# Two neighbouring positions per partition, attention in 64x64 array tiles, state product on the diagonal

## The chip, the cores and the metric

The kernel runs on one core of one Trainium2 chip. Its time is device microseconds, the median over runs. The core has five engines with queues of their own, each executed in order: PE (matrix products, with weight loads that the profile lists as PEld), DVE and ACT (elementwise work; both read PSUM), POOL (elementwise work in SBUF, and DMA issue), SP (DMA issue). They wait for one another through semaphores.

## The reference

Inputs are q, k, v of shape (4 batches, 8 heads, 768 positions, 64), one decay `lam` per head, and the weights of a two-layer network. Attention is linear with decay, and is written in blocks of 64 positions:

```python
Dmask = np.where(rel >= 0, lam[:, None, None] ** rel[None, :, :], 0.0)
...
intra = np.einsum('bhic,bhjc->bhij', qb, kb) * Dmask[None]
intra = np.einsum('bhij,bhjd->bhid', intra, vb)
inter = np.einsum('bhid,bhde->bhie', qb * lam_pow[None], kv_state)
out[:, :, sl] = intra + inter
...
kv_state = lam_block[None, :, None, None] * kv_state + np.einsum('bhsd,bhse->bhde', kb_dec, vb)
```

The result is laid out as 3072 tokens of 512 values, x, and goes through

```python
h = x @ w_in                                            # 512 -> 2048
g = np.maximum(h, 0.0) + alpha * np.minimum(h, 0.0)
return (g @ w_out).astype(np.float32)                   # 2048 -> 512
```

The block size doesn't change the result, so a kernel may take 128 positions at a time.

## The kernel before, in words

A chunk is 128 positions of all four batches, 512 tokens; there are six chunks (`sb` or `c`), and 24 units of one chunk and one batch. Heads go in pairs: two heads of 64 values fill 128 partitions, `hp` counts pairs and `hl` the head in the pair.

For each unit, `load` (L63) brings q, k and v with one position per partition, so that each partition takes eight pieces of 256 bytes, one per head. `casts` (L185) makes fp16 copies on the engines that a three-letter word names for q, k, v (A for ACT, V for DVE, G for POOL) and lets POOL make `kdec`, the decayed k. `transposes` (L204) turns k and q by eight PE transposes into one PSUM tile, copies it to `qkT`, and POOL makes the decayed queries `qdT`. `scores` (L219) is eight products of k and q into two PSUM tiles; DVE multiplies them by the decay mask into `sm` (L235). `outputs` (L238) is eight inter products of the state `R` with `qdT` (L245) and eight intra products of v with `sm` (L255) into one PSUM tile, which ACT copies to `xT`. `states` (L267) is eight products of `kdec` and v (L283); POOL scales the old state into `rd` (L273) and DVE adds (L294).

`up` (L300) makes one block of 128 of the 2048 hidden values for 512 tokens, or for half of them: four matmuls into `h_ps`, of which there are three buffers, then ACT's `m` (L314) and DVE's `g` (L317). `down` (L326) adds four of sixteen matmuls for 128 tokens into `o_ps`; after the last, ACT copies and issues the store (L343).

Nothing is reordered: the queue of each engine is the order of the calls from L399 on. That order is written by hand for chunk 0, up(0), chunk 1's attention and up(1); then `weave` (L386) mixes chunk 2's attention with down(0), and from there attention of chunk c+1 with up(c) and down(c-1). The weights `w_in` and `w_out` come in four pieces each, issued on POOL's queue and cast to fp16 on the way. Two small transfers on SP's queue, `gate` (L90), wait for a piece of the weights and so hold back the loads of chunk 1 and of chunks 2 on. PSUM has eight banks: one for transposes, two for scores, one for `ot`, one shared by `o_ps` and the state product, three for `h_ps`.

Of the kernel before, what the change touches and what calls it, by code (L numbers as in the profile page):

```python
# [11 lines left out]
def kernel(  # L12
# [10 lines left out]
):  # L23
    nc = tc.nc
# [10 lines left out]
    NSB = S // L  # L35
# [4 lines left out]
    D2 = 2 * D  # L40
    CH = B * L

    const = ctx.enter_context(tc.tile_pool(name="const", bufs=1))
    raw_pool = ctx.enter_context(tc.tile_pool(name="raw", bufs=6))
# [8 lines left out]
    h_ps_pool = ctx.enter_context(tc.tile_pool(name="hps", bufs=3, space=bass.MemoryType.PSUM))  # L53

# [5 lines left out]
    )  # L60
    raws = {}

    def load(sb, b):  # L63
        raws[sb, b] = []
        for n, src in zip("qkv", (q, k, v)):
            t = raw_pool.tile([128, DM], fp32, tag=f"{n}raw", name=f"{n}raw")
            nc.sync.dma_start(  # L67
                out=t.rearrange("p (h d) -> p h d", h=H),
                in_=src[b, :, ds(sb * L, L), :].rearrange("h s d -> s h d"),
            )  # L70
            raws[sb, b].append(t)
# [18 lines left out]
    def gate(i, w):  # L90

        nc.sync.dma_start(out=gates[:, i : i + 1], in_=w)

    load(0, 0)
    alpha_sb = const.tile([128, NF], fp32, name="alpha_sb")
    load(0, 1)
    nc.sync.dma_start(out=alpha_sb, in_=moe_alpha.rearrange("(t p) -> p t", p=128))
    load(0, 2)
    load(0, 3)


# [5 lines left out]
    make_identity(nc, ident)  # L107

    rel_i = const.tile([128, L], int32, name="rel_i")
    nc.gpsimd.iota(rel_i, pattern=[[1, L]], base=0, channel_multiplier=-1)  # L110
    rel_f = const.tile([128, L], fp32, name="rel_f")
    nc.vector.tensor_scalar(out=rel_f, in0=rel_i, scalar1=0.0, scalar2=None, op0=ALU.max)
    rev_i = const.tile([128, 1], int32, name="rev_i")
    nc.gpsimd.iota(rev_i, pattern=[[0, 1]], base=L - 1, channel_multiplier=-1)
    rev_f = const.tile([128, 1], fp32, name="rev_f")
    nc.vector.tensor_copy(out=rev_f, in_=rev_i)
    pos_i = const.tile([128, L], int32, name="pos_i")
    nc.gpsimd.iota(pos_i, pattern=[[1, L]], base=1, channel_multiplier=0)
    pos_f = const.tile([128, L], fp32, name="pos_f")
    nc.vector.tensor_copy(out=pos_f, in_=pos_i)  # L120
# [8 lines left out]
    dmask = const.tile([128, 2, NHP, L], fp32, name="dmask")  # L129
    for hl in range(2):  # L130
        nc.vector.tensor_tensor(
            out=dmask[:, hl],
            in0=rel_f.unsqueeze(1).to_broadcast([128, NHP, L]),
            in1=llv[:, hl, :].unsqueeze(2).to_broadcast([128, NHP, L]),
            op=ALU.mult,
        )
        nc.scalar.activation(dmask[:, hl], dmask[:, hl], AF.Exp)
        nc.gpsimd.affine_select(
            out=dmask[:, hl],
            in_=dmask[:, hl],  # L140
            compare_op=ALU.is_ge,
            fill=0.0,
            base=0,
            pattern=[[0, NHP], [1, L]],
            channel_multiplier=-1,
        )
    kdecay = const.tile([128, H], fp32, name="kdecay")
    nc.scalar.activation(kdecay, loglam, AF.Exp, scale=rev_f[:, :])
# [4 lines left out]
    qdecay = const.tile([128, NHP, L], fp32, name="qdecay")  # L153
    rdecay = const.tile([128, NHP], fp32, name="rdecay")
    oma = const.tile([128, NF], fp32, name="oma")

    def late_constants():
        nc.vector.tensor_tensor(
            out=qdecay,
            in0=pos_f.unsqueeze(1).to_broadcast([128, NHP, L]),  # L160
            in1=llp.unsqueeze(2).to_broadcast([128, NHP, L]),
            op=ALU.mult,
        )
        nc.scalar.activation(qdecay, qdecay, AF.Exp)
        nc.scalar.activation(rdecay, llp, AF.Exp, scale=float(L))
        nc.vector.tensor_scalar(
            out=oma, in0=alpha_sb, scalar1=-1.0, scalar2=1.0, op0=ALU.mult, op1=ALU.add
        )


    R = [const.tile([128, NHP, D], fp16, name=f"R{b}") for b in range(B)]


    T = {}
    XT = {}

# [8 lines left out]
    def casts(sb, b, eng):  # L185
        qr, kr, vr = raws.pop((sb, b))
        q16 = half_pool.tile([128, DM], fp16, tag="q16", name="q16")
        k16 = half_pool.tile([128, DM], fp16, tag="k16", name="k16")
        v16 = half_pool.tile([128, DM], fp16, tag="v16", name="v16")
        copy_on(eng[0], q16, qr)  # L190
        copy_on(eng[1], k16, kr)
        copy_on(eng[2], v16, vr)
        T[sb, b] = dict(q16=q16, k16=k16, v16=v16)
        if sb < NSB - 1:
            kdec = half_pool.tile([128, DM], fp16, tag="kdec", name="kdec")
            nc.gpsimd.tensor_tensor(  # L196
                out=kdec.rearrange("p (h d) -> p h d", h=H),
                in0=kr.rearrange("p (h d) -> p h d", h=H),
                in1=kdecay.unsqueeze(2).to_broadcast([128, H, D]),
                op=ALU.mult,  # L200
            )
            T[sb, b]["kdec"] = kdec

    def transposes(sb, b, eng):  # L204
        t = T[sb, b]
        tp = ps.tile([128, 2, NHP, L], fp16, tag="tk", name="tp")
        for hp in range(NHP):
            nc.tensor.transpose(tp[:, 1, hp, :], t["k16"][:, ts(hp, D2)], ident)  # L208
        for hp in range(NHP):
            nc.tensor.transpose(tp[:, 0, hp, :], t["q16"][:, ts(hp, D2)], ident)  # L210
        qkT = qkt_pool.tile([128, 2, NHP, L], fp16, tag="qkT", name="qkT")
        copy_on(eng, qkT, tp)
        t["qkT"] = qkT
        if sb > 0:
            qdT = qkt_pool.tile([128, NHP, L], fp16, tag="qdT", name="qdT")
            nc.gpsimd.tensor_tensor(out=qdT, in0=qkT[:, 0], in1=qdecay, op=ALU.mult)  # L216
            t["qdT"] = qdT

    def scores(sb, b):  # L219
        t = T[sb, b]  # L220
        s = [ps.tile([128, NHP, L], fp32, tag=f"s{hl}", name=f"s{hl}") for hl in range(2)]
        for hp in range(NHP):
            for hl in range(2):
                p = ds(hl * 64, 64)
                nc.tensor.matmul(  # L225
                    s[hl][:, hp, :],
                    lhsT=t["qkT"][p, 1, hp, :],
                    rhs=t["qkT"][p, 0, hp, :],
                    start=True,
                    stop=True,  # L230
                )
        t["sm"] = []
        for hl in range(2):
            sm = sm_pool.tile([128, NHP, L], fp16, tag=f"sm{hl}", name=f"sm{hl}")
            nc.vector.tensor_tensor(out=sm, in0=s[hl], in1=dmask[:, hl], op=ALU.mult)  # L235
            t["sm"].append(sm)

    def outputs(sb, b):  # L238
        t = T[sb, b]
        ot = ps.tile([128, NHP, L], fp32, tag="ot", name="ot")  # L240
        if sb > 0:
# [287 lines left out]
```

## Time and profile before

| | |
|---|---|
| median of 3 runs (lowest, highest) | 247.75 us (246.79, 247.91) |
| span of the profiled execution, first to last instruction | 244.7 us |
| the profiled execution's own time | not listed; the median less the span is 3.05 us |
| PE busy | 217.8 us, 1728 matmuls |
| DVE, ACT, POOL busy | 124.7, 112.4, 86.3 us |
| input queue (SP) | 18.89 MB in 76948 packets, 41.5% of 16 engines' span |
| output queue (ACT) | 6.30 MB in 3744 packets, 7.1% |
| weights (POOL's queue) | 4224 packets, 4.19 MB, 11.3% |

The profile is one execution. A busy share is an average over stages, so the prediction reads stretches of the span. In the timeline a line is: start, length from first start to last end, engine, line of the kernel, operation, output and inputs, shape, and how many instructions are merged. Matmuls overlap, so the length of a merged line is not the sum of its parts. The chain of waits is followed back from the last instruction to what released each step.

### The profile page before, as it was taken

The numbers are of one execution on the slowest core, as the hardware profiler recorded it, in microseconds if no ns is written. First come the engines' busy times: TensorE is split into PE (matmuls) and PEld (weight loads), VectorE is DVE, ScalarE is ACT, GpSimd is POOL, SyncE is SP. The second block draws the span as 40 slices with busy tenths as digits, with TensorE's granted clock in tenths as the row PEclk, the third lists the DMA queues.
The fourth block names the chain that finished last, engine by engine and source line by source line (L and its number), as shares of the span: only waits on it lengthen the run. The fifth ranks groups of instructions, "written<-read, shape, count | busy, mean of one in ns | idle before, by whom it ended". The sixth has DMA issues, their size and how long they took to land.

```text
span 244.7 us, 4422 instructions
## 1 busy us (share of the span) xinstructions
PE 217.8 (89%) x1728; PEld 110.9 (45%) x1728; DVE 124.7 (51%) x205; ACT 112.4 (46%) x200; POOL 86.3 (35%) x119
## 2 busy tenths in 40 slices
PE   0529597989997998999999999999999999999994
PEld 0316443556443444444444444444444444444453
DVE  3534476768862334566456565556565534444100
ACT  4427667856642324534434535435534443444211
POOL 1823317992058684515641614611330100000000
PEclk9999999999999999999999999999999999999999
DMA  6999699799999999999304901101101100111122
GB/s 140 153 218 196 101 229 218 130 133 183 187 203 246 248 226 260 197 255 220 96 2 119 228 3 43 43 3 43 43 3 43 46 24 20 43 43 46 43 86 86
DMA packets 84936, 29.65 MB, mean 121 GB/s; under 512 B 77620, under 2 KB 81972, under 8 KB 84916
## 3 DMA queue, kind: packets, MB, share of 16 engines
q1 hardware_dynamic: 76948, 18.89, 41.5%
q0 software_dynamic: 4224, 4.19, 11.3%
q10 hardware_dynamic: 3744, 6.30, 7.1%
q8 instruction: 13, 0.21, 0.4%
q14 instruction: 7, 0.06, 0.1%
HBM read 27.28 MB, written 6.29 MB: 137 GB/s over the span
## 4 chain that ended last, share of the span: by engine, by line
PE 67%; DMA 11%; POOL 8%; SPq 5%; ACT 3%; issue 3%; DVE 1%; ACTq 0%; POOLq 0%
PE o_ps L332 27%; PE h_ps L305 25%; DMA vraw<-in_v_dram 9%; PE o_ps L355 6%; SPq L67 5%; DMA w_in_sb<-in_moe_w_in_dram 2%; POOL kdec L196 2%; PE ot L245 2%; PE ot L255 2%; PE s L225 2%; POOL qdT L216 2%; POOL v L183 1%; ACT o_sb L345 1%; PE tp L210 1%; PE kv L283 1%
## 5 line engine op out<-in xcount | busy, mean ns | idle before, releaser
L317 DVE SCALAR_TENSOR_TENSOR g<-m,oma,h_ps 128x512 f16<-128x512 f32 (+1 forms) x108 | 73.6, 687 | 73.0 <-ACT m L314 71.4
L305 PE MATMUL h_ps<-xT,w_in_sb 128*128 128x512 f16 (+1 forms) x432 | 98.0, 359 | 2.8 <-ACT xT L265 1.8
L314 ACT ACTIVATE m<-h_ps 128x512 f32<-128x512 f32 (+1 forms) x108 | 59.4, 550 | 76.2 <-PE h_ps L305 75.4
L332 PE MATMUL o_ps<-w_out_sb,g 128*128 128x512 f16 x320 | 82.2, 380 | 0.4 <-ACT o_sb L345 0.2
L305 PEld LDWEIGHTS <-w_in_sb 128*128 128x128 f16 x432 | 40.1, 99 | 39.3 <-issue 3.6
L216 POOL TENSOR_TENSOR qdT<-qkT,qdecay 128x512 f16<-128x512 f16 x20 | 23.2, 1164 | 67.0 <-DVE qkT L181 65.2
L332 PEld LDWEIGHTS <-g 128*128 128x128 f16 x320 | 28.8, 98 | 32.5 <-issue 0.8
L235 DVE TENSOR_TENSOR sm<-s,dmask 128x512 f16<-128x512 f32 x48 | 30.8, 684 | 12.9 <-PE s L225 12.9
L345 ACT ACTIVATE o_sb<-o_ps 128x512 f32<-128x512 f32 (+1 forms) x25 | 14.5, 580 | 26.6 <-PE o_ps L332 15.5
L208 PE MATMUL tp<-ident,k 128*128 128x128 f16 x96 | 10.0, 230 | 13.5 <-DVE k L181 12.0
L196 POOL TENSOR_TENSOR kdec<-kraw,kdecay 128x512 f16<-128x512 f32 x20 | 20.8, 1042 | 0.0
L265 ACT ACTIVATE xT<-ot 128x512 f16<-128x512 f32 x24 | 14.3, 597 | 13.9 <-PE ot L255 12.8
L183 POOL CAST v<-vraw 128x512 f16<-128x512 f32 x24 | 14.7, 614 | 14.3 <-DMA vraw<-in_v_dram 12.5
L183 POOL CAST k<-kraw 128x512 f16<-128x512 f32 x20 | 12.2, 611 | 18.1 <-DMA kraw<-in_k_dram 18.1
L208 PEld LDWEIGHTS <-k 128*128 128x128 f16 x96 | 7.2, 102 | 18.9 <-DVE k L181 12.1
L179 ACT ACTIVATE q<-qraw 128x512 f16<-128x512 f32 x23 | 14.0, 623 | 1.8 <-DMA qraw<-in_q_dram 1.8
L181 DVE COPY qkT<-tp 128x1024 f16<-128x1024 f16 x18 | 12.4, 690 | 4.5 <-PE tp L210 4.4
L355 PE MATMUL o_ps<-w_out_sb,g 128*128 128x512 f16 (+1 forms) x80 | 14.0, 336 | 0.0
L225 PE MATMUL s<-qkT 64*128 64x128 f16 x192 | 10.2, 229 | 2.5 <-ACT qkT L179 1.5
L255 PE MATMUL ot<-sm,v 128*64 128x128 f16 x192 | 10.8, 236 | 1.1 <-DVE sm L235 1.1
L210 PE MATMUL tp<-ident,q 128*128 128x128 f16 x96 | 10.1, 231 | 1.8 <-ACT q L179 1.6
L225 PEld LDWEIGHTS <-qkT 64*128 64x128 f16 x192 | 5.8, 98 | 11.2 <-issue 6.4
(44 smaller groups left out, 90.0 us busy)
## 6 DMA issues: line engine op xcount, KB each, us to landing
qraw<-in_q_dram SPq DMA_DIRECT2D x24, 256.0 KB, 5.2
kraw<-in_k_dram SPq DMA_DIRECT2D x24, 256.0 KB, 5.2
vraw<-in_v_dram SPq DMA_DIRECT2D x24, 256.0 KB, 5.1
out_dram<-o_sb ACTq DMA_DIRECT2D x23, 256.0 KB, 2.0
w_in_sb<-in_moe_w_in_dram POOLq DMA_DIRECT2D x4, 512.0 KB, 6.3
w_out_sb<-in_moe_w_out_dram POOLq DMA_DIRECT2D x4, 512.0 KB, 7.2
out_dram<-o_sb ACTq DMA_DIRECT2D x2, 128.0 KB, 1.7
lam_sb<-in_lam_dram ACTq DMA_DIRECT2D x1, 4.0 KB, 3.5
```

What stands on the lines that cost most here:

```text
L183: nc.gpsimd.tensor_copy(out=out, in_=in_)
L196: nc.gpsimd.tensor_tensor(out=kdec.rearrange("p (h d) -> p h d", h=H), in0=kr.rearrange("p (h d) -> p h d", h=H), in1=kdecay.unsqueeze(2). ...
L208: nc.tensor.transpose(tp[:, 1, hp, :], t["k16"][:, ts(hp, D2)], ident)
L216: nc.gpsimd.tensor_tensor(out=qdT, in0=qkT[:, 0], in1=qdecay, op=ALU.mult)
L225: nc.tensor.matmul(s[hl][:, hp, :], lhsT=t["qkT"][p, 1, hp, :], rhs=t["qkT"][p, 0, hp, :], start=True, stop=True,)
L235: nc.vector.tensor_tensor(out=sm, in0=s[hl], in1=dmask[:, hl], op=ALU.mult)
L305: nc.tensor.matmul(h_ps[:, 0:n], lhsT=w_in_sb[:, gi, ts(f, 128)], rhs=XT[c][:, gi, cols], start=(gi == 0), stop=(gi == NHP - 1),)
L314: nc.scalar.activation(m[:, 0:n], h_ps[:, 0:n], AF.Relu, scale=-1.0)
L317: nc.vector.scalar_tensor_tensor(out=G[c, f][:, cols], in0=m[:, 0:n], scalar=oma[:, f : f + 1], in1=h_ps[:, 0:n], op0=ALU.mult, op1=ALU.add,)
L332: nc.tensor.matmul(o_ps, lhsT=G[c, f][:, ts(t, 128)], rhs=w_out_sb[:, f, :], start=(f == 0), stop=(f == NF - 1),)
L345: nc.scalar.activation(o_sb[:, 0:n], o_ps[:, 0:n], AF.Copy)
L355: nc.tensor.matmul(o_ps[:, 0:n], lhsT=G[c, f][:, ts(t, 128)], rhs=w_out_sb[:, f, ts(x, n)], start=(f == 0), stop=(f == NF - 1),)
```

## The change

A partition now holds two neighbouring positions, so a load takes pieces of 512 bytes. Loads and the three letters of `casts` now go in the order k, q, v. A chunk is 256 positions of two batches (still 512 tokens; chunk c is positions 256(c // 2) on, of batches 2(c % 2) and the next), and a unit is four heads of 256 positions of one batch: 24 units again, numbered through, four to a chunk. `e` is the parity of a position, `a` the half of the unit (128 positions, 64 partitions). Scores, intra and the state product are each done as 16 products of 64 partitions and 64 output rows, which fall into the four 64x64 tiles of the array. The state of each 128 positions is kept in a tile of its own, and two states are copied by POOL onto the diagonal of a zeroed 128x128 tile `RD`, so that the inter product is four full-width matmuls. `cluster(old, new)` puts inter of the unit before, scores of the new one, intra of the unit before and the state product of the new one next to each other; `ot` and `kv` share two PSUM banks, `acc`, and `h_ps` has two banks instead of three, to which up adds the bank of `o_ps` for each third step before down starts. The mask is made by ACT per head and multiplied by POOL with a 0/1 tile; half of it is made later, after unit 1's casts. `oma` comes from `alpha` through a PE transpose. In the hand-written part, ACT no longer copies `qkT` (all six such copies go to DVE), and up is done in halves for ten and twelve blocks of chunks 0 and 1, where it was four and eight.

```diff
-    raw_pool = ctx.enter_context(tc.tile_pool(name="raw", bufs=6))
+    raw_pool = ctx.enter_context(tc.tile_pool(name="raw", bufs=5))
...
-    h_ps_pool = ctx.enter_context(tc.tile_pool(name="hps", bufs=3, space=bass.MemoryType.PSUM))
+    h_ps_pool = ctx.enter_context(tc.tile_pool(name="hps", bufs=2, space=bass.MemoryType.PSUM))
...
+                nc.sync.dma_start(
+                    out=t[:, ds(x * n, n), :],
+                    in_=src[b, ds(x * n, n), ds(pb * W, W), :].rearrange("h (p e) d -> p h (e d)", e=2),
+                )
...
+    for t in RD.values():
+        nc.vector.memset(t, 0.0)
...
+    def decay_mask(hp):
+        for hl in range(2):
+            h = 2 * hp + hl
+            nc.scalar.activation(dmask[:, hl, hp], rel_f, AF.Exp, scale=loglam[:, h : h + 1])
+            nc.gpsimd.tensor_tensor(out=dmask[:, hl, hp], in0=dmask[:, hl, hp], in1=keep, op=ALU.mult)
...
+    def slopes():
+        at = h_ps_pool.tile([128, CH], fp32, tag="h", name="at_ps")
+        nc.tensor.transpose(at[:, 0:NF], alpha_sb, ident32)
...
+            for e in range(2):
+                nc.gpsimd.tensor_tensor(
+                    out=kdec[:, e],
...
+    def cluster(old, new):
+        acc = ps.tile([128, 2, 512], fp32, tag="acc", name="acc")
...
+                for hp in range(2):
                     nc.tensor.matmul(
-                        ot[p, hp, :],
-                        lhsT=R[b][p, hp, :],
-                        rhs=t["qdT"][p, hp, :],
+                        ot[a][:, hp, :].rearrange("p (e j) -> p e j", e=2),
+                        lhsT=RD[bb, ho][:, a, hp].rearrange("p h d -> p (h d)"),
+                        rhs=to["qdT"][:, hp, :, ds(a * 64, 64)],
...
+                    for a, hl in QUADS:
+                        p = ds(hl * 64, 64)
+                        nc.tensor.matmul(
+                            s[hl][ds(a * 64, 64), hp, e, :].rearrange("p (e j) -> p e j", e=2),
+                            lhsT=t["qkT"][p, 1, hp, e, ds(a * 64, 64)],
+                            rhs=t["qkT"][p, 0, hp, :, ds(a * 64, 64)],
...
+                    for hl, a in QUADS:
+                        p = ds(a * 64, 64)
+                        nc.tensor.matmul(
+                            ot[a][ds(hl * 64, 64), hp, :],
+                            lhsT=to["v16"][p, e, 2 * hp + hl, :],
+                            rhs=to["sm"][hl][p, hp, e, :],
...
+                            nc.tensor.matmul(
+                                kv[a][ds(hl * 64, 64), hp, :],
+                                lhsT=t["kdec"][p, e, 2 * hp + hl, :],
+                                rhs=t["v16"][p, e, 2 * hp + hl, :],
...
+                if n == 0:
+                    nc.vector.tensor_copy(out=after, in_=kv[a])
+                    continue
+                for hp in range(2):
+                    nc.vector.scalar_tensor_tensor(
+                        out=after[:, hp],
+                        in0=R[b, hh, n][:, hp],
...
+                    nc.gpsimd.tensor_copy(out=RD[b, hh][p, a, :, hl, :], in_=R[b, hh, 2 * pb + a][p])
...
+        if third and n_up % 3 == 0:
+            h_ps = ps.tile([128, CH], fp32, tag="op", name="h_ps")
...
+            lambda: (casts(u, "GAG"), casts(u + 1, "GAG")),
+            lambda: transposes(u, "V"),
+            lambda: cluster(None, u),
+        ]
+        for x in range(u + 1, u + 4):
+            steps.append(lambda x=x: (transposes(x, "V"), casts(x + 1, "GAG") if x < u + 3 else None))
+            steps.append(lambda x=x: cluster(x - 1, x))
+        steps.append(lambda: cluster(u + 3, None))
...
+    casts(1, "AAG")
+    load_win(1)
+    decay_mask(2)
+    decay_mask(3)
...
+    transposes(1, "V")
+    cluster(0, 1)
+    slopes()
+    cluster(1, None)
+    casts(2, "VAG")
     load_win(2)
...
+    for f in range(4):
+        up(0, f, 0, True)
+    casts(3, "VAG")
     load_win(3)
+    transposes(2, "V")
+    cluster(None, 2)
+    transposes(3, "V")
+    for f in range(4, 8):
+        up(0, f, 0, True)
+    cluster(2, 3)
+    for f in range(8, 10):
+        up(0, f, 0, True)
+    cluster(3, None)
+    for f in range(10):
+        up(0, f, 1, True)
...
+    casts(4, "GAG")
+    casts(5, "GAG")
+    transposes(4, "V")
+    up(0, 14, None, True)
+    cluster(None, 4)
+    transposes(5, "V")
+    up(0, 15, None, True)
+    cluster(4, 5)
     load_wout(0)
+    cluster(5, None)
...
+    transposes(6, "V")
+    for f in range(6, 8):
+        up(1, f, 0, True)
+    cluster(None, 6)
     load_wout(2)
     load_wout(3)
+    transposes(7, "V")
+    for f in range(8, 10):
+        up(1, f, 0, True)
+    cluster(6, 7)
+    for f in range(10, 12):
+        up(1, f, 0, True)
+    cluster(7, None)
+    for f in range(12):
+        up(1, f, 1, True)
```

## The prediction

> **What bounds the kernel now.** Read the slices first: TensorE is full from about 90 us to the end, and the DMA row is full up to about 90 us. The stretches put numbers on it.
>
> ```profile
> PE   0529597989997998999999999999999999999994
> DMA  6999699799999999999304901101101100111122
> ```
>
> ```profile
> core 0: us, PE busy (x) PEld busy (x) DVE busy (x) ACT busy (x) POOL busy (x), PEclk, DMA share, GB/s
> 0.00:21.00 21.00, 6.74 (x81) 4.76 (x82) 8.38 (x21) 9.08 (x16) 8.32 (x19) 1.00 1.01 179
> 21.00:36.80 15.80, 13.32 (x110) 8.05 (x109) 10.03 (x18) 10.35 (x23) 4.66 (x7) 1.00 0.99 165
> 36.80:56.60 19.80, 16.50 (x214) 9.87 (x213) 13.75 (x26) 14.49 (x26) 17.77 (x23) 1.00 1.05 160
> 56.60:67.60 11.00, 10.77 (x68) 6.28 (x66) 8.99 (x18) 7.25 (x15) 0.61 (x1) 1.00 1.08 189
> 67.60:92.80 25.20, 22.56 (x226) 11.08 (x225) 11.01 (x18) 7.50 (x13) 18.76 (x25) 1.00 1.13 232
> 165.20:227.60 62.40, 62.08 (x385) 29.12 (x384) 31.24 (x46) 28.38 (x48) 6.87 (x8) 1.00 0.09 35
> ```
>
> The reader is to see five stages. Start: the first up matmul is at 20.97 us. Stage 2, to the end of up(1): 46.6 us, PE busy 40.6, DVE 32.8. Stage 3, chunk 2's attention with down(0): 25.2 us. Stage 4, 92.8 to 227.6: PE never idle. Tail 17.1 us. The span is 244.7; the median of the runs is 247.75, so 3.05 us lie around the span, and I add them to every sum (the profiled run's own time isn't listed). A measurement of this kernel tells about 0.5%, 1.2 us, from no change.
>
> Next the timeline, in stage 4, for the price of attention on PE:
>
> ```profile
> 137.63 0.41 PE L245 MATMUL ot<-qdT,R 64*64 64x128 f16 x8
> 137.97 0.41 PE L255 MATMUL ot<-sm,v 128*64 128x128 f16 x8
> 138.32 1.04 PE L305 MATMUL h_ps<-xT,w_in_sb 128*128 128x512 f16 x4
> 142.31 0.32 PE L283 MATMUL kv<-v,kdec 128*64 128x64 f16 x8
> ```
>
> Eight matmuls of 128 columns occupy 0.34 us from start to next start, of which about 0.1 is the change of tile shape (where shape doesn't change, 91.36 to 91.60 in the same view, it is 0.24). A matmul's own duration there is 222 ns, so starts lie (0.41-0.222)/7 = 27 ns apart: two tiles already run together. kv at 64 columns: (0.32-0.205)/7 = 16 ns, the closest spacing shown; its weight loads are 12 ns apart.
>
> Last the chain of waits, for half-width up steps:
>
> ```profile
> 56.65 0.56 PE h_ps L305 x4
> 57.65 0.49 DVE g L317
> 58.19 0.61 PE h_ps L305 x4
> 59.24 0.49 DVE g L317
> ```
>
> Three halves per 1.58 us, 0.53 each (PE needs 0.45): they turn round three PSUM buffers through ACT and DVE.
>
> **The change, part by part.**
>
> *Rows of 512 bytes.* The input queue moved 18.89 MB in 41.5% of the span, 186 GB/s; the output queue, 2 KB rows, 6.30 MB in 7.1%, 362 GB/s. Those are my ends; per-row cost linear between them gives about 257 GB/s, so a chunk (3.1 MB) takes 12 us, not 17. The Trainium skill ("DMA: Bandwidth & Descriptors", Specifications) puts the least transfer for line rate at 512 B, which would be the fast end. Either way the sum is the same: by the walk below every chunk lands before PE reaches it (chunk 1 issued at about 29, needed at 44; chunk 2 issued at 69, needed at 79), so what is late next isn't data.
>
> *Start: 20.9 (20.97 before).* POOL carries it. ACT's table load ends at 6.06; four mask products (0.57 each by the 616 ns of 128x256 rd) end at 8.95; v 0.56, kdec 1.14, w_in issue 0.85: 11.5; two RD copies 0.45 and qdT 1.16: 13.1; v, kdec, w_in again: 15.65; four more masks: 17.95; DVE's sm 1.28 and state copy 0.25, with qdT(1) 1.16 beside them, and RD 0.45: 19.55; inter and intra 0.6, xT 0.6: 20.9. Bounds: 18.5 if the second masks hide, 22 if POOL's strided reads cost. The RD memsets, the extra iotas and the alpha transpose lie beside this chain: the first two ahead of lam's landing (4.34), the last while PE waits for the second masks; the alpha load that SP issued for 1.13 us becomes 16 rows, off the chain too. Prices not in the trace are lines through two sizes of the nearest row: a 256-wide POOL product 0.616 less the 0.05 by which its operations overlap; an RD copy 0.22, between iota's 0.236 and memset's 0.205 at 128 columns; R's copy 0.25, from the 128x128 cast's 0.227 (for each 0.17 to 0.42, as the smallest and the 256-wide rows stand).
>
> *PE per unit.* Before: transposes 0.47, scores 0.33+0.09, inter 0.34+0.09, intra 0.35, kv 0.25+0.09: 2.01. After: transposes 0.47; inter 4 full-width matmuls, 0.23; shape in and out 0.2; scores and intra 16 each at 16 ns, 0.26 each; kv 16 at 12 ns, 0.20. Sum 1.62. Bounds: four tiles ideally together (14, 14, 7 ns) 1.46; still only two (28, 28, 16) 2.06. I take the spacing rows, which are nearest. The tiling page of the Trainium skill ("TensorEngine Tiling (Array Packing)", Restrictions and Gotchas) speaks against this: column tiling gives up Fast Weight Load. kv's loads are column-tiled now and 12 ns apart; if the rule cost scores' loads their whole 0.26 again, a unit would be 1.88.
>
> *Stage 4: 19.3 of attention instead of 24.0.* Up and down are 128 groups of 0.866, 110.8, unchanged. Before, 134.8-110.8 = 24.0. After, chunk 3: 4x1.62 plus 0.2 for a fifth cluster, 6.7; chunks 4 and 5 have half the kv, 6.3 each. DVE gains 0.7 a unit (four R steps of 0.28 against one of 0.42) and POOL 0.2 (four RD copies 0.85 for rd 0.62; kdec in halves 1.14 for 1.04): both idle over 40% here, 20.1 and 15.9 busy of 36.2, so this costs nothing while clusters stay 6 us apart and an RD is due only one cluster later. Two h_ps buffers instead of three cost nothing here: up(f+2) starts 3.5 us after up(f), whose evacuation takes 0.60+0.75 and at worst stands behind sm and four R steps (1.28+1.1).
>
> *Stage 3: 21.4 instead of 25.2.* Sixteen down groups 13.9, four units 6.7, xT at the end and one RD wait 0.8. Before had 2.6 us of PE idle on DMA and qdT.
>
> *Stage 2: 57.9 instead of 46.6.* PE work: 44 halves x 0.53 = 23.3 (24 before), 10 full x 0.87 = 8.7, six units 9.7: 41.7. Then the waits, from the queue orders; rows: sm 2x0.64, qkT on DVE 0.69, R in this stage 0.25+2x0.28 (0.28 by the line through 478 ns at 256 and 747 at 512), g 0.45 half, 0.75 full:
> - cold clock: four halves at 0.89, the spacing at 20.97 to 22.75: 1.4 (the granted clock reads 1.0 there, the durations don't).
> - qkT(2) behind four g and a k cast on DVE, scores(2) behind it: 1.7.
> - up 7 waits for g 4, which is behind sm(2), R(2), qkT(3): 1.3.
> - cluster(3,None): PE has nothing else while DVE does sm(3), R(3), 1.0; then xT and its latency 0.85 before the next up.
> - q(4) is cast on ACT behind m 13: 1.0.
> - cluster(4,5): DVE has g 14, sm(4), R(4), qkT(5), 3.5, against 1.4 of transposes and up 15: 2.1.
> - cluster(5,None): g 15, sm, R 2.1, xT 0.85.
> - cluster(6,7) 1.4; cluster(7,None) 1.6 and xT 0.85.
> Together 16.2. POOL's w_out(2) moves from 53.6 to about 63, behind RD(6); the gate on SP and chunk 2's loads come 7 us later and are still in time. The bound from below is DVE's own work: 44x0.45+10x0.75 + 6x2.77 + casts 0.9 = 45; from above, the walk with 28 ns tiles, about 60.
>
> *Sum:* 20.9+57.9+21.4+110.8+19.3+17.1 = 247.4; with 3.05, 250.4: 1.1% slower.
>
> **Rivals.**
> 1. Stage 2 flows (other side). If PE waits no more than the 6.0 us it idles there now (46.6-40.6), stage 2 is 47.8 and the time 240.3. For: operations of the same kinds fitted before, with DVE at 70%. Against: before, ACT made six qkT copies (1.02 each) and the chunk-0 R, and up steps stood between scores and outputs; now DVE does it all, and four clusters have nothing beside them. It decides at 13.4 us of waits: below that the kernel is faster.
> 2. Packing fails: two tiles at a time, 2.06 a unit, 0.44 x 22 units (two of the 24 lie in the start) less what waits hide, +8: 258. For: the drain of 0.1 at each shape change. Against: kv's 16 ns shows that PE issues pairs that fast.
> 3. The rows don't help at all (DMA stays at 186 GB/s). Chunk 1 then lands at 29+17 = 46 for the second batch, needed at 57: no cost; chunk 2's first batch at 69+9 = 78 against 79: still about 250 to 251. This rival is priced the same, so the time can't tell it; the queue's busy share can.
>
> **How the numbers follow.** Waits as walked, with packing: 0.50, 250.4, own range 247 to 254. Rival 1 and cases between: 0.33, 240 to 246.5. Rival 2: 0.12. Rival 3: 0.05. Range 240.5 to 256. Faster than 246.5: 0.34; within 1.2 us: 0.15 (the lower edge of the main case and the upper of rival 1); slower: 0.51.
>
> **What would show it.** First up near 21 us; PE slices from 21 to 79 us at 7 tenths with DVE at 8 or more; idle before up and cluster matmuls put down to DVE and xT, 14 to 18 us in all; up(1) ending at 77 to 80; a stretch of up, down and attention taking 34.5 us where 36.2 stood; the input queue's share at 23 to 31%. The forecast is wrong if up(1) ends before 74, or if attention on PE stays at 2 us a unit.

## The result, and the profile after

| | before | after |
|---|---|---|
| median of 4 runs (lowest, highest) | 247.83 us (246.79, 248.55) | 255.36 us (253.75, 256.68) |
| ratio, with its 95% interval | | 1.030 (1.024 to 1.036): slower |
| the profiled execution of after: time, span | | 256.11, 254.0 us |

The sign and the range of the forecast held (250.4, 240.5 to 256.0); the loss was under-sized, 1.1% for 3.0%, and 255.36 lies above the walked case's own range, 247 to 254. The page of after opens with the slices: busy tenths of PE, then the granted TensorE clock and the share of the DMA engines.

```profile
PE   0445669749687989699999999999999999999994
PEclk9999999977999999799999999999999999999999
DMA  5994997016899999999101110111011101111122
```

The reader is to see two dips in the clock row that the page of before does not have: in slices 9 and 10 (51 to 63 us), and in slice 17 (102 to 108 us). In the first slice of each the PE row dips too. The DMA row is full from 70 to 120 us. (Other executions of before do lose some clock: of the eleven beside e12, seven have a mean clock of 0.993 and took 246.9 to 248.9 us, four have 1.000 and took 245.5 to 246.9.)

The stretches of after, in the columns in which the prediction showed those of before (busy time and instruction count of PE, PEld, DVE, ACT, POOL; granted clock, DMA share, GB/s), cut at the same events:

```profile
0.00:22.82 22.82, 6.20 (x118) 4.37 (x118) 10.26 (x33) 9.99 (x22) 17.28 (x37) 1.00 0.85 185
22.82:81.43 58.61, 44.24 (x568) 29.94 (x565) 42.27 (x91) 30.67 (x69) 28.58 (x49) 0.94 0.74 148
81.43:106.77 25.34, 21.56 (x305) 11.72 (x305) 10.98 (x28) 5.62 (x10) 18.60 (x37) 0.97 1.11 299
106.77:236.44 129.67, 129.67 (x1170) 66.03 (x1169) 75.08 (x132) 60.91 (x104) 52.33 (x105) 0.99 0.19 61
```

| | before | forecast | after | after less forecast |
|---|---|---|---|---|
| start, to the first up matmul | 20.97 | 20.9 | 22.82 | +1.9 |
| stage 2, to the first down matmul | 46.6 | 57.9 | 58.61 | +0.7 |
| stage 3, to the next up matmul | 25.2 | 21.4 | 25.34 | +3.9 |
| stage 4, to the last four down groups | 134.8 | 130.1 | 129.67 | -0.4 |
| tail | 17.1 | 17.1 | 17.56 | +0.5 |
| around the span | 3.05 | 3.05 | 2.1 | -0.95 |
| together (before: the median; after: the profiled run) | 247.75 | 250.4 | 256.1 | +5.7 |

So the loss of 9.3 us of span is stage 2's +12 and the start's +1.9, less 5 us won in stage 4. Stage 3 won nothing. The medians differ by 7.5 us, since the profiled execution of before was one of its faster. Where time and span of one execution of before are both listed they lie 1.7 us apart (246.33 and 244.6, beside e1), so the 3.05 around the span, a median less the span of a faster execution, was too much.

Stage 4, from the timeline: one unit, with its transposes three groups earlier.

```profile
117.27 0.39 PE L235 MATMUL tp<-ident,k 128*128 128x128 f16 x4
117.49 0.39 PE L235 MATMUL tp<-ident,q 128*128 128x128 f16 x4
117.72 1.03 PE L380 MATMUL h_ps<-xT,w_in_sb 128*128 128x512 f16 x4
...
120.31 0.39 PE L275 MATMUL acc<-qdT,RD 128*128 128x128 f16 x4
120.62 0.42 PE L292 MATMUL s<-qkT 64*64 64x128 f16 x16
120.87 0.39 PE L304 MATMUL acc<-sm,v 64*64 64x128 f16 x16
121.09 0.29 PE L319 MATMUL acc<-v,kdec 64*64 64x64 f16 x16
121.32 1.04 PE L410 MATMUL o_ps<-w_out_sb,g 128*128 128x512 f16 x4
```

From start to start: transposes 0.45, state product 0.31, scores 0.25, outputs 0.22, kv 0.23, together 1.46 us a unit, where before took 2.01. Sixteen 128-column products pass in 0.25 us; one after the other at 0.42 ns a column (a full-width matmul of 512 columns takes 216 ns) they would take 0.86. The tiles run side by side.

Stage 2, from PE's timeline: five of its waits, in brackets with what ended each: the first for g 4, the next three before state products, the last before the first down matmul.

```profile
32.13 0.60 PE L380 MATMUL h_ps<-xT,w_in_sb 128*128 128x256 f16 x4 [1.10 <-DVE g L397]
...
35.82 0.29 PE L275 MATMUL acc<-qdT,RD 128*128 128x128 f16 x2 [1.30 <-POOL RD L364]
...
51.77 0.28 PE L275 MATMUL acc<-qdT,RD 128*128 128x128 f16 x2 [1.62 <-POOL RD L364]
...
54.93 0.40 PE L275 MATMUL acc<-qdT,RD 128*128 128x128 f16 x2 [1.99 <-POOL RD L364]
55.26 0.64 PE L304 MATMUL acc<-sm,v 64*64 64x128 f16 x16
...
81.43 1.89 PE L410 MATMUL o_ps<-w_out_sb,g 128*128 128x512 f16 x8 [1.47 <-DVE g L397]
```

The last one is the price of a borrowed bank: the last up step of the stage, its 54th, is a third step, so its `h_ps` lies in the bank of `o_ps`, and the first down matmul waits until its g is made. In the gap that ends at 54.93 the clock falls, and it stays low to 60.7 us. Stretches of 2 us; the last three columns are granted clock, DMA share, GB/s:

```profile
50.00:52.00 2.00, 0.38 (x3) 0.11 (x2) 1.96 (x6) 0.60 (x1) 0.58 (x2) 1.00 0.00 0
52.00:54.00 2.00, 0.82 (x50) 0.65 (x48) 2.00 (x5) 0.60 (x1) 1.16 (x1) 0.96 0.00 0
54.00:56.00 2.00, 1.07 (x19) 0.67 (x20) 0.65 (x3) 0.05 (x1) 1.66 (x4) 0.50 0.00 0
56.00:58.00 2.00, 1.84 (x9) 1.16 (x8) 0.11 (x1) 1.85 (x4) 2.00 (x5) 0.50 0.85 73
58.00:60.00 2.00, 2.00 (x12) 1.40 (x10) 1.33 (x3) 0.99 (x3) 2.00 (x4) 0.50 1.17 197
```

Stage 3, ACT's timeline (ACTq L426 is the issue of an output store):

```profile
91.30 0.60 ACT L423 ACTIVATE o_sb<-o_ps 128x512 f32<-128x512 f32 x1 [0.32 <-PE o_ps L410]
94.29 0.34 ACTq L426 DMA_DIRECT2D out_dram<-o_sb  x1
94.68 0.63 ACT L203 ACTIVATE q<-qraw 128x512 f16<-128x512 f32 x1 [2.78 <-DMA kraw<-in_k_dram]
95.28 0.60 ACT L337 ACTIVATE xT<-acc 128x512 f16<-128x512 f32 x1
97.07 0.60 ACT L423 ACTIVATE o_sb<-o_ps 128x512 f32<-128x512 f32 x1 [1.19 <-PE o_ps L410]
102.28 0.35 ACTq L426 DMA_DIRECT2D out_dram<-o_sb  x1
102.67 0.60 ACT L337 ACTIVATE xT<-acc 128x512 f16<-128x512 f32 x1 [5.01 <-DMA qraw<-in_q_dram]
```

The result in `o_sb` was ready at 97.7, its store was issued at 102.28, and what ended the wait is an input transfer that has nothing to do with it. Behind it stand xT, DVE's state sum (which writes the bank that xT reads) and PE, idle for 2.38 us. The chain of waits shows the same pair:

```profile
85.49 8.67 DMA kraw<-in_k_dram
94.16 8.05 DMA qraw<-in_q_dram
...
102.67 0.61 ACT xT L337
103.31 0.86 DVE R L351 x4
104.31 0.50 PE acc L275 x4
```

Why a store waits for a load is in the program's list of instructions, not in the trace: each transfer of SP and ACT is given one of eight completion counters in turn, and before it is issued it waits until the transfer that had the counter last has landed. The second store of stage 3, the load before it on counter 4 (k of chunk 3, second batch), then the third store and its load (q of chunk 4, first batch), as listed, each with its place in its engine's queue:

```
91 L426 DMACopy out_0_dram<-o_sb_1637 128x512 [waits DMAHW4_49,Activation_49]
28 L87 DMACopy kraw_1389<-in_k_dram 128x8x128 [waits DMAHW4_49,Pool_49]
95 L426 DMACopy out_0_dram<-o_sb_1747 128x512 [waits DMAHW1_49,Activation_49]
32 L87 DMACopy qraw_1874<-in_q_dram 128x8x128 [waits DMAHW1_49,Activation_49]
```

### The profile page after: what moved, and what is told of

It reads as the page before. It is cut to its first block, busy times and chain, and to the rows that moved or that the text cites. A ratio compares the mean times of both kernels' runs of the same rounds, so it can differ in the third digit from the quotient of the medians.

```text
span 254.0 us, 5553 instructions
## 1 busy us (share of the span) xinstructions
PE 215.7 (85%) x2233; PEld 119.8 (47%) x2233; DVE 139.3 (55%) x284; ACT 110.3 (43%) x210; POOL 116.8 (46%) x225
## 3 DMA queue, kind: packets, MB, share of 16 engines
q1 hardware_dynamic: 37524, 18.89, 28.6%
## 4 chain that ended last, share of the span: by engine, by line
PE 68%; POOL 9%; DMA 8%; DVE 6%; ACT 4%; issue 3%; ACTq 0%; POOLq 0%; DVEq 0%
PE h_ps L380 30%; PE o_ps L410 24%; PE o_ps L433 5%; DMA kraw<-in_k_dram 3%; DMA qraw<-in_q_dram 3%; DVE g L397 2%; PE tp L235 2%; POOL qdT L250 2%; POOL dmask L171 2%; PE acc L304 2%; ACT m L388 2%; PE s L292 2%; PE acc L275 2%; DMA lam_sb<-in_lam_dram 2%; POOL RD L364 1%
## 5 line engine op out<-in xcount | busy, mean ns | idle before, releaser
L380 PEld LDWEIGHTS <-w_in_sb 128*128 128x128 f16 x472 | 46.6, 102 | 41.4 <-issue 6.7
L250 POOL TENSOR_TENSOR qdT<-qkT,qdecay 128x512 f16<-128x512 f16 x24 | 27.9, 1162 | 42.0 <-DVE qkT L205 41.7
L364 POOL COPY RD<-R 64x128 f16<-64x128 f16 x80 | 23.6, 294 | 28.3 <-DVE R L351 19.5
L337 ACT ACTIVATE xT<-acc 128x512 f16<-128x512 f32 x24 | 14.3, 597 | 36.6 <-PE acc L319 18.9
L221 POOL TENSOR_TENSOR kdec<-kraw,kdecay 128x256 f16<-128x256 f32 x48 | 28.5, 613 | 0.0
L275 PE MATMUL acc<-qdT,RD 128*128 128x128 f16 x80 | 9.0, 226 | 16.0 <-POOL RD L364 12.2
L205 DVE COPY qkT<-tp 128x1024 f16<-128x1024 f16 x24 | 16.5, 687 | 5.7 <-PE tp L235 5.6
L275 PEld LDWEIGHTS <-RD 128*128 128x128 f16 x80 | 6.0, 98 | 22.0 <-POOL RD L364 14.5
L207 POOL CAST k<-kraw 128x512 f16<-128x512 f32 x20 | 12.2, 609 | 8.0 <-DMA kraw<-in_k_dram 7.7
L351 DVE SCALAR_TENSOR_TENSOR R<-R,rdecay,acc 128x64 f16<-128x64 f16 x64 | 14.3, 275 | 2.6 <-ACT xT L337 2.2
L292 PE MATMUL s<-qkT 64*64 64x128 f16 x384 | 10.5, 229 | 2.8 <-DVE qkT L205 2.5
## 6 DMA issues: line engine op xcount, KB each, us to landing
out_dram<-o_sb ACTq DMA_DIRECT2D x23, 256.0 KB, 2.0
kraw<-in_k_dram SPq DMA_DIRECT2D x2, 256.0 KB, 5.2
qraw<-in_q_dram SPq DMA_DIRECT2D x2, 256.0 KB, 6.1
```

The costliest lines, as they stand in the source:

```text
L205: nc.vector.tensor_copy(out=out, in_=in_)
L207: nc.gpsimd.tensor_copy(out=out, in_=in_)
L221: nc.gpsimd.tensor_tensor(out=kdec[:, e], in0=kr[:, e], in1=kdecay[:, ds(4 * hh, 4), e].unsqueeze(2).to_broadcast([128, 4, D]), op=ALU.mult,)
L250: nc.gpsimd.tensor_tensor(out=qdT, in0=t["qkT"][:, 0], in1=qdecay[:, ds(2 * hh, 2), :].rearrange("p h (e j) -> p h e j", e=2), op=ALU.mult,)
L275: nc.tensor.matmul(ot[a][:, hp, :].rearrange("p (e j) -> p e j", e=2), lhsT=RD[bb, ho][:, a, hp].rearrange("p h d -> p (h d)"), rhs=to["qd ...
L364: nc.gpsimd.tensor_copy(out=RD[b, hh][p, a, :, hl, :], in_=R[b, hh, 2 * pb + a][p])
```

## The experiments

Theory A, at first: stage 2 is long because of DVE's queue and an order that leaves PE empty-handed, stage 3 because of stores held behind loads, the start because of POOL's masks. Rival B: the small tiles and the changes of tile shape are dear. Rival C: the transfers (512-byte rows, 512 KB pieces) land late. Kernels named e1 to e7 and e11 to e15 change after in the way shown. Each was timed beside the kernel before on its chip; times are medians, and ratios are to before.

**e1: loads of chunk 3 later.**

```diff
-    for c in (2, 3):
-        for bi in range(2):
-            load(c, bi)
+    for bi in range(2):
+        load(2, bi)
...
-        if c + 2 < NC:
-            for bi in range(2):
-                load(c + 2, bi)
+        for d in ((3, 4) if c == 2 else (c + 2,)):
+            if d < NC:
+                for bi in range(2):
+                    load(d, bi)
```

> Chunk 3's loads are issued after chunk 2's attention instead of ahead of it. Theory A (stage 3 lost 4 us because ACT's output stores stand behind input transfers that are still queued, and xT and the state product stand behind those stores): the stores of stage 3 go out at once, PE's idle time of 2.4 us at about 104 us and the low granted clock after it go, stage 3 falls from 25.5 to about 21.5 us, the time from 255.4 to 251.5. Theory B (the small array tiles and their shape changes are what is dearer): no change, 255. Theory C (transfers land too late): slower, because chunk 3 now lands later, 256 or more.

Measured: 256.22 us (1.035, 1.027 to 1.043), as after. Stage 3 took 25.13, and ACT was held 2.7 and 4.8 us by the same two loads. The edit was empty: SP has only loads in its queue, so where they stand in the program changes neither when SP issues them nor the counters. It tells nothing between the theories.

**e2: qkT on ACT**, for units 2 to 7 alike.

```diff
-    transposes(2, "V")
+    transposes(2, "A")
...
```

> The copies of the transposed k and q out of PSUM, units 2 to 7, run on ACT (where the kernel before had them) instead of DVE. Theory A (stage 2 is paced by DVE's queue, 42.3 us busy of 58.6): DVE loses six copies of 0.69, 4.1 us, ACT gains six of about 1.0; stage 2 falls by 2 to 5 us, the time to 250.5 to 253.5. Theory B or C (tiles or transfers set stage 2): no change, 255; if ACT's queue is as tight as DVE's, slower by up to 2.

Measured: 254.06 us (1.026, 1.020 to 1.032). DVE's busy time in stage 2 fell from 42.3 to 39.2, and stage 2 grew from 58.6 to 60.7 (its mean granted clock fell to 0.89). That part of theory A falls: the 3 us less on DVE bought nothing, so the sum of DVE's work isn't the pace. (How much ACT's copies cost by themselves stays open: PE's busy time rose by 2.8 us with the lower clock.) ACT's copy takes 1.03 where DVE's takes 0.69, and PE waits for each result in turn. What the whole won came from stage 3, 22.56, where ACT was held only 1.6 and 3.0 us, since it began 2.1 us later and its loads only 1.1.

**e3: rows of 256 bytes.** Each load is two, one for each parity of the position.

```diff
...
-                    out=t[:, ds(x * n, n), :],
-                    in_=src[b, ds(x * n, n), ds(pb * W, W), :].rearrange("h (p e) d -> p h (e d)", e=2),
+                    out=t[:, e, ds(x * n, n), :],
+                    in_=src[b, ds(x * n, n), ds(pb * W, W), :].rearrange("h (p e) d -> e p h d", e=2)[e],
...
```

> Each load is split by the position's parity into two with 256-byte pieces, as long as the rows before; all else stays, so this undoes the row length alone (and doubles the number of transfers). Theory A (the row length shortens transfers that PE does not wait for in stage 2, and matters only where stores stand behind loads): the input queue's share goes from 28.6% back to about 40%, stage 2 stays within 1 us of 58.6, stage 3 is 0 to 5 us longer by the held stores, the time 255 to 260. Theory C (transfers pace the first 107 us): stage 2 longer by 5 us or more, the time 262 or more.

Measured: 251.36 us (1.014, 1.008 to 1.020), 4 us under after, where I had expected 0 to 5 us more. The queue's share went to 36.4%, stage 2 stayed at 58.87; the gain is 1.1 in the start (lam is in use at 3.7 instead of 5.05 us), 3.1 in stage 3 and 0.85 of low clock at the beginning of stage 4. Rival C falls for stage 2. Why stage 3 gains was open: shorter rows, smaller pieces, or other counters.

**e5: products of one tile one after the other.** The order of the loops alone.

```diff
-            for hp in range(2):
-                for e in range(2):
-                    for a, hl in QUADS:
+            for a, hl in QUADS:
+                for hp in range(2):
+                    for e in range(2):
...
```

> The same small matmuls of scores, outputs and state, ordered so that the four (or eight) on one tile of the array follow one another; so consecutive ones can't run beside each other. Theory A (packing works: 16 scores in 0.42 us, starts 13 ns apart; PE gains 0.5 us a unit by it): at 0.42 ns a column (512 columns take 216 ns) a 128-column matmul alone takes 54 ns, so scores and outputs take 0.85 us each instead of 0.25, kv 0.43 instead of 0.2: +1.4 us a unit, stage 4 (12 units) from 129.6 to about 145, the whole 278 to 288. Theory B (the tiles hardly overlap and are dear already): stage 4 up by less than 4 us, the whole under 265.

Measured: 256.15 us (1.031, 1.022 to 1.039), as after; stage 4 129.56. My expectation was wrong by 15 us in stage 4, but not in favour of rival B. A scores batch of e5, then kv:

```profile
115.92 0.45 PE L292 MATMUL s<-qkT 64*64 64x128 f16 x16
116.17 0.34 PE L319 MATMUL acc<-v,kdec 64*64 64x64 f16 x16
```

Sixteen products still pass in 0.25 us, four on one tile after another or not, and 0.86 would be needed one by one. So the tiles run beside each other however their products are ordered within sixteen; how the array holds four for one tile while it starts the next was not tried.

**e11: 512-byte rows in pieces of 256 KB**, to part pieces from rows.

```diff
-    def load(c, bi, halves=1):
+    def load(c, bi, halves=2):
```

> The rows stay 512 bytes, but each load is split in two by heads (0 to 3, 4 to 7), so that the pieces have the size of e3's (256 KB) and come in the order in which units use them. Theory P (it is the size and number of the queued pieces, not the length of the rows, that holds back the start and stage 3: a store on ACT stands behind an input transfer several issues earlier, and a smaller one lands sooner): first up matmul at about 21.7 instead of 22.8, stage 3 about 22.2 instead of 25.3 us, the input queue's share stays at 28 to 29%, the time 250.5 to 252. Rival R (the 512-byte rows themselves are worse, because they crowd other transfers): no change, 254.5 to 256.

Measured: 258.50 us (1.046, 1.039 to 1.053), slower than after by 3 us. Theory P falls: smaller pieces land sooner (5.2 to 5.3 us after issue for 7.2 to 7.6), yet the stores of stage 3 drew counters whose loads landed late, and ACT was held three times:

```profile
89.29 0.63 ACT L203 ACTIVATE q<-qraw 128x512 f16<-128x512 f32 x1 [3.19 <-DMA kraw<-in_k_dram]
...
98.75 0.63 ACT L203 ACTIVATE q<-qraw 128x512 f16<-128x512 f32 x1 [6.88 <-DMA kraw<-in_k_dram]
...
106.33 0.60 ACT L337 ACTIVATE xT<-acc 128x512 f16<-128x512 f32 x1 [5.97 <-DMA vraw<-in_v_dram]
```

Stage 3 took 29.23. The start stayed at 22.77, where theory P had 21.7.

**e4: no copies of the state onto the diagonal.**

```diff
-                for hl in range(2):
-                    p = ds(hl * 64, 64)
-                    nc.gpsimd.tensor_copy(out=RD[b, hh][p, a, :, hl, :], in_=R[b, hh, 2 * pb + a][p])
```

> POOL's copies of the state onto the diagonal (80 of 294 ns) are left out; the state product's matmuls stay and read the zeros of the memset, so the output lacks the contribution of earlier blocks. This prices the copies and the waits on them. Theory A: about 0.7 us in the start (one pair on the way to the first up), 1 to 3 us in stage 2, where clusters find nothing else to run, 0 to 1 in stage 3; nothing in stage 4: the time 250.5 to 253.5. Rival (POOL's copies are hidden by the state's own sums on DVE and by xT): 254.5 to 256.

Measured: 249.73 us (1.013, 1.006 to 1.020). The start fell by 1.3, stage 2 by only 0.5: PE waited there for sums and masks that end just before the copies would. Stage 3 fell to 21.66, but its stores drew other counters too and ACT was held 4.0 us at one place that hurt nobody, so this fall is not the price of the copies.

**e6: another order in stage 2.** Nothing but the order of the calls, from the first clusters on; the core of it:

```diff
-    up(0, 15, None, True)
+    up(0, 12, None, True)
     cluster(4, 5)
     load_wout(0)
+    up(0, 13, None, True)
+    up(0, 14, None, True)
     cluster(5, None)
+    up(0, 15, None, True)
...
-    for f in range(8, 10):
+    for f in range(6, 8):
         up(1, f, 0, True)
     cluster(6, 7)
-    for f in range(10, 12):
+    for f in range(8, 11):
         up(1, f, 0, True)
     cluster(7, None)
+    up(1, 11, 0, True)
...
```

> Only the order of the part of the program from the first cluster to the end of up(1) is changed: a few up steps are put between a unit's transposes and its cluster, and one to three between a cluster and the next, so that PE has work while DVE, ACT and POOL make its operands. Theory A (stage 2 is long because PE stands empty-handed in an order written out by hand, not because of the tiles or of an engine's sum): stage 2 from 58.6 to 50 to 53 us, PE's granted clock stays at 1.00 in it, the time 247 to 250. Theory D (DVE's sum of 42.3 us and the round of m and g set the pace): stage 2 not under 56, the time 253 to 256.

Measured: 248.78 us (1.009, 1.005 to 1.013). Stage 2 52.43; with the start (23.49, which took over unit 2's transposes) 5.5 us less to its end, the mean granted clock there 0.97 for 0.94, not the 1.00 of my expectation. The waits before the state products are now 0.2 to 0.9 us. This is the larger part of the loss, and it is in the order, not in the tiles.

**e7: second masks on DVE.**

```diff
-    decay_mask(2)
-    decay_mask(3)
     query_decay(2)
     query_decay(3)
     transposes(1, "V")
+    decay_mask(2, nc.vector)
+    decay_mask(3, nc.vector)
...
```

> The second four mask products move from POOL (724 ns each) to DVE, after unit 1's transposes are copied out. Theory A (the start is POOL's chain): POOL is free 2.9 us sooner, DVE takes about 0.35 to 0.5 each, and the first up matmul falls from 22.8 to 20.5 to 21.5 us; stage 2 stays, the time 253 to 254.5. Rival (the start is set by the landing of the loads and by ACT's exponentials): no change, 255 to 256.

Measured: 254.16 us (1.029, 1.022 to 1.036); the start 20.63, 2.2 less, stage 2 58.68. DVE took 0.83 for each mask, about twice what I had put.

**e12: stores of stage 3 issued by SP.**

```diff
-        nc.scalar.dma_start(out=rows, in_=o_sb[:, 0:n])
+        (nc.sync if c == 0 else nc.scalar).dma_start(out=rows, in_=o_sb[:, 0:n])
```

> Only the four output stores of stage 3 (chunk 0) are issued by SP, behind the loads of chunks 2 and 3, instead of by ACT; nothing on the path waits for a store. Theory S (ACT is held at its stores: each transfer of SP and ACT takes one of eight completion counters in turn and waits until the last transfer with that counter has landed, here an input load; xT, the state and the next cluster stand behind): ACT's waits for kraw and qraw in stage 3 go, PE's 2.4 us idle before the state product at 104 and the low granted clock after it too; stage 3 falls from 25.3 to 21.4 to 22.2, stage 4 by up to 0.9, the time 250.5 to 252. Rival (the transfers themselves, still crowded, hold PE): stage 3 stays over 24 us and the time at 255.

Measured: 251.04 us (1.015, 1.009 to 1.021). Stage 3 22.18, stage 4 128.85, clock 1.00 in both. The place where after was held 5 us, on e12's ACT:

```profile
96.24 0.60 ACT L423 ACTIVATE o_sb<-o_ps 128x512 f32<-128x512 f32 x1 [1.19 <-PE o_ps L410]
99.33 0.60 ACT L337 ACTIVATE xT<-acc 128x512 f16<-128x512 f32 x1 [2.49 <-PE acc L319]
102.03 0.60 ACT L337 ACTIVATE xT<-acc 128x512 f16<-128x512 f32 x1 [2.10 <-PE acc L304]
```

There ACT now waits for PE, not PE for ACT. Theory S is shown. The rival falls too: the transfers of e12's stage 3 are lighter (DMA share 0.84, after 1.11), but in e13, below, the share is 1.11 again and the stage still takes 22.19. The other runs line up: ACT held by input loads for 0 us, stage 3 22.2 (e12, e14, e15); 0.6 and 1.0 us, 22.2 (e3, e13); 4.6 us, 22.6 (e2); 7.5 to 7.8 us, 24.4 to 25.7 (e1, e6, e7, after); 16.0 us, 29.2 (e11). e4, without the copies, was held 4.0 us and took 21.7.

**e13: e12 with the pieces of e3.**

> The stores of e12 and the 256-byte pieces of e3 together. Theory S (e3's gain in stage 3 was the luck of which loads the stores' counters fell on, and e3's gain in the start was lam landing earlier, 3.7 instead of 5.05 us): start 21.7, stage 3 within 0.6 us of e12's, the time 0.5 to 1.5 us below e12's. Rival R (shorter rows make stage 3 itself shorter): stage 3 shorter than e12's by over 1 us. Rival C (with stores out of the way the longer rows show their worth): e13 slower than e12.

Measured: 250.32 us (1.012, 1.006 to 1.017; 249.93 to 250.86), e12 250.88 to 251.97 on the same chip. Start 21.55, stage 3 22.19. So with no store held by a load, short and long rows take the same time in stage 3, and e3's gain there was that its stores drew counters that held them little. Otherwise e3's edit gives lam's earlier landing alone, and that is in favour of the short rows, or of the first load's smaller pieces, which e3 halves too.

**e14: e6, e7 and e12 together**, with unit 2's k and q cast by ACT while it is idle.

```diff
+    casts(2, "AA-", 0)
     cluster(0, 1)
     slopes()
+    transposes(2, "V")
     cluster(1, None)
-    casts(2, "VAG")
+    casts(2, "--G")
...
```

> The order of e6, the second masks on DVE as in e7, the stores of stage 3 on SP as in e12, and unit 2's k and q cast by ACT while it is idle in the start. Theory (the change's loss is three separate queues and none of it is in the new tiles): start 20.5 to 21.3, stage 2 51.5 to 53, stage 3 21.4 to 22.2, stage 4 128.8, tail 17.6; the span about 241.5, the time 241.5 to 245, below the kernel before by 1 to 2.5%. If the gains overlap (the same waits counted twice), 245.5 to 248.

Measured: 244.32 us (244.27 to 244.47), 0.987 of before (0.982 to 0.992), so 0.8 to 1.8% less. Part of this is the clock, which before keeps at 1.000 in only four of the eleven executions beside it (245.5 to 246.9 us). Its page:

```profile
PE   0366798787998899999999999999999999999993
PEclk9999999999999999999999999999999999999999
```

```profile
0.00:20.32 20.32, 7.37 (x125) 5.14 (x125) 13.50 (x37) 11.02 (x24) 14.34 (x32) 1.00 0.89 194
20.32:73.66 53.34, 43.60 (x561) 29.64 (x557) 41.70 (x90) 29.75 (x68) 29.01 (x50) 1.00 0.84 169
73.66:95.85 22.19, 20.75 (x305) 11.54 (x305) 10.89 (x28) 5.42 (x10) 17.86 (x37) 1.00 0.83 216
95.85:224.70 128.85, 128.85 (x1169) 65.76 (x1168) 75.07 (x132) 60.89 (x104) 52.96 (x106) 1.00 0.28 83
```

The gains add up (5.5 of e6, 2.2 of e7 and 4.0 of e12 make 11.7 us; the span is 11.5 shorter than after's), and the clock row shows no fall. The row doesn't tell all, though:

```profile
29.50 0.64 PE L294 MATMUL s<-qkT 64*64 64x128 f16 x16
45.96 0.42 PE L294 MATMUL s<-qkT 64*64 64x128 f16 x16
```

The first of these batches has the long duration of the low stretches (0.64, as at 55.26 us in after). In e14 the durations stay long up to about 31 us, in after up to 26.5. So something is left to win between 20 and 31 us, where e14 has a gap of 2.45 us at 23.3.

**e15: four more edits in the start of e14:** the first load in pieces of 256 bytes, unit 1's v on ACT with one mask on POOL, unit 1's state copies on ACT, unit 3's k on ACT.

> e14 with four more edits in the start: the first load in 256-byte pieces (so that lam, which waits among its packets, lands at 3.7 instead of 5.0 us), one of the second masks on POOL ahead of its v and state work, unit 1's v cast and its state copies onto the diagonal on ACT, unit 3's k cast on ACT. Theory: the start is a chain from lam's landing over ACT, POOL and DVE, each late by the one before: first up matmul from 20.3 to 18.8 to 19.5, stage 2 from 53.3 to 52 to 53.5, the time 242 to 243.5. Rival (the first loads or unit 1's data set the start, not lam): start above 20, the time 244 to 245.

Measured: 243.42 us (241.42 to 244.28), 0.985 of before (0.978 to 0.991). The first up is at 18.68, 1.6 earlier, but stage 2 took 54.68: in the profiled run (244.28) the clock was low between 41 and 48 us. Runs with a mean clock of 0.999 to 1.000 took 241.4 to 242.4. e14 ran on another chip; the two intervals overlap, so that e15 is faster than e14 isn't shown.

## Why the prediction was right and wrong

**Start, 20.9 forecast, 22.82 measured: the sizes on POOL, and lam.** The chain was right, POOL to its end. Eight masks had been priced at 0.57 from the 128x256 `rd`; four took 2.78, 0.70 each: +1.0 over eight. (They read fp32 where `rd` reads fp16; whether that is the reason wasn't tried.) A copy onto the diagonal had been 0.22; it took 294 ns, 0.6 a pair: +0.3. lam was in use at 5.05 instead of 4.34: +0.7. The upper bound of 22 was too low. e7 gave back 2.2 by the masks alone, e3 1.1: lam was in use 1.3 earlier there, and POOL's first mask began 1.3 earlier.

**PE per unit, 1.62 forecast, 1.46 measured.** The spacing taken from kv's row (16 ns) was too wide; starts came 13 ns apart, (0.42-0.229)/15. Rival 2 (packing fails) is out. The weighing of the page "TensorEngine Tiling (Array Packing)" of the Trainium skill came out for the trace: a loss of fast weight loads to column tiles does not show in these 0.25 us.

**Stage 4, 130.1 forecast, 129.67 measured:** right, the lower unit price and 0.8 of low clock taken together (128.85 without it). Two `h_ps` banks, four state sums and POOL's copies cost nothing there, as walked.

**Stage 2, 57.9 forecast, 58.61 measured.** The waits came where they were walked: for the 1.7, 1.3, 1.0, 1.0, 2.1, 2.1, 1.4 and 1.6 forecast, PE's timeline has 1.48, 1.10, 1.30, 0.98, 1.62, 1.99, 0.91 and 1.15, 10.5 for 12.2. The total came so near partly by luck. These waits were 1.7 shorter than walked, those for xT 1.5 shorter (1.1 for 2.55). In their place came two terms that the walk lacked: 1.47 for the bank of `o_ps` before the first down matmul, and the clock: 22 matmuls of half steps after 56.6 took 4.54 us where DVE's round of 0.53 for four makes 2.9, so 1.6 us. The bound from below was misnamed as DVE's own work (45; it was busy 42.3): e2 took 3 us off DVE and won nothing in the stage. Rival 1, which I gave 0.33, was right in its mechanism, not for this kernel: with up steps between scores and outputs (e6) the stage takes 52.4, still above the 47.8 which it priced.

**Stage 3, 21.4 forecast, 25.34 measured: the step that failed.** The prediction said of the rows that every chunk lands before PE reaches it, "so what is late next isn't data". PE did find its data. But the loads were still in flight when ACT had to issue stores, and the stores wait for loads; the sum for the stage had no term for this. I had looked for who needs the data of a transfer, not for who needs its counter. With the stores on SP the stage takes 22.18, 3.2 less: 2.4 of PE's wait and 0.8 of low clock. The 0.8 that is left over the forecast is mostly idle time of PE (1.43, where 0.8 was walked). So the 3.0 us which stage 3 could have won against before (22.2 for 25.2; four units at 0.55 are 2.2 of it) were taken by a new wait. That the time stayed below 256.0 all the same is luck: this end of the range was there for rival 2, whose cause is out.

**The rows** were priced at nothing, with 257 GB/s as guess for the queue: 18.89 MB in 28.6% of 254.0 us are 260 GB/s. Rival 3 gave the same time, as said; the share tells that the longer rows did shorten the transfers, and e13 that this buys no time.

**The sum:** start +1.9, stage 2 +0.7, stage 3 +3.9, stage 4 -0.4, tail +0.5, around the span -0.95: +5.7 for the profiled run, +5.0 for the median.

## What to carry to other kernels

When a change regroups the work, price the order as well as the operations: here 5.5 us were lost because clusters stood back to back with nothing for PE in between, and were won back without touching an operation. For every transfer on a queue ask not only who needs its data, but which later instruction waits for its counter, and on which engine that one stands in line; an idle issuing engine is the place for stores. And the time PE stands idle can cost twice, by the wait and by the clock after it.

## What was unexpected of the hardware

- In after the granted clock fell to 0.50 at 53.9 us, where gaps of 1.62 and 1.99 us have 1.2 us of small products between them, and at 105.1 us, behind a gap of 2.38 us; it stayed there for 6.8 and 3.4 us. In e6 a gap of 2.45 us (at 26.5 us) was followed by a fall and one of 2.23 us (96.4 us) was not, nor was one of 2.21 us in e11 (97.2 us). So the length of a gap alone doesn't decide it. The Trainium skill ("TensorE: Matmul & The Clock Gate", Part 1) puts the fall to half after an idle window of about 3.4 us. The half agrees; the gaps here were shorter.
- The clock row reads 1.00 in the start too, where the durations are those of the low stretches: sixteen products take 0.64 us up to 26.5 us in after, and 0.42 later.
- Input rows of 512 bytes moved 260 GB/s over their queue's time; 256-byte pieces in the same kernel 18.89 MB in 36.4% of 249.1 us, 208 GB/s; output rows of 2 KB 6.30 MB in 6.7%, 370 GB/s. The least size for line rate, 512 B in "DMA: Bandwidth & Descriptors" (Specifications) of the Trainium skill, was not enough for the rate of the 2 KB rows. Those go the other way, though, from the core to memory, and no run here has input rows of 2 KB.
- The 4 KB of lam were in use at 5.05 us beside loads with 512-byte rows and at 3.7 us beside the same loads in 256-byte pieces, where the first load's transfers are also half as large. Which of the two it is, and how, wasn't tried.
- On DVE a product of a mask with the 0/1 tile (128x256, fp32) took 0.83 us, on POOL 0.72 (medians of four each in e7).
